# Another order for the attention's steps and for the second MoE stage's first block, the last rows' gate on TensorE, and 11 fewer idle transposes

## The chip, the core and the metric

The kernel runs on one core of one Trainium2 chip. The metric is the device time of one execution in microseconds (us). The core has five engines that run side by side: TensorE (PE in the rows; its weight loads, PEld, have a row of their own), VectorE (DVE), ScalarE (ACT), GpSimd (POOL) and SyncE (SP), which here only issues transfers. Each takes its instructions in the order in which the program lists them and waits for the others through semaphores. Sixteen DMA engines move data.

## The reference

The output of an attention feeds a mixture of experts, whose output feeds a second one:

```python
q_rot, k_rot = rotate(q), rotate(k)           # 4 batches, 8 heads, 576 rows, 64 wide
scores = scale * matmul(q_rot, k_rot.T); scores -= max(scores)
attn = exp(scores); attn /= sum(attn) + 1e-09
x = matmul(attn, v)                           # reordered to 2304 rows of 512

logits = x @ w_gate + modality_bias[modality_id]      # first stage, 8 experts
e = argmax(logits); gate_w = softmax(logits)[e]
x = gate_w * (relu(x @ w1[e]) @ w2[e])                # w1 512x1024, w2 1024x512

do_compute = x @ w_skip > 0                           # second stage
logits = x @ w_gate2; e = argmax(logits); gate_w = softmax(logits)[e]
out = x + where(do_compute, gate_w * (relu(x @ w1_2[e]) @ w2_2[e]), 0)
```

All of it is float32.

## The kernel before, in words

Nearly every product is made of three matmuls: each operand is split into a high and a low part, and high x high, low x high and high x low are added. ScalarE writes the high part (a cast), VectorE the low part (a subtraction); the steps ending in `_hi` and `_lo` and the pieces `split1`, `split2` are these. The low part waits for the high part, and TensorE for both.

**Attention** (`attention`, lines 268 to 690). There are 16 pairs of heads, p = 0 to 15. A pair is loaded, rotated (`rope`, VectorE and GpSimd), transposed (`qk_tr`, L364 and L367), split and stacked. Its scores come in tiles of 128 rows by 576 columns: `s_mm` (L430, four or eight matmuls, two buffers S), `s_max` (L443, VectorE), `s_exp` (L447, ScalarE). The weights of a tile are transposed (`t_mm`, L525) and split (`t_hi` L528, `t_lo` L532), then multiplied with v (`pv`, L559). The finished output O of a head is copied by ScalarE (`o_ev`, L568), turned (`o_mm`, L577), divided by the row sums (`o_norm`, L583; `r_inv`, L480 to L482) and stored (`x_store`, L590 and L592). a and b are the two heads of a pair. After each batch come the routing steps of the first MoE stage (`route…`, `scat…`, which write the experts' lists).

Each step has a position in the table `POS` (L39 to L83). A pair's base is 10 p; all steps of all pairs are sorted by base plus position and issued in that order, so a step's number sets its place in the queue of every engine that it uses. One step may hold several instructions on several queues; a tuple gives one number for each instruction of a TensorE step. The steps at the end of the last pair are already those of the first MoE stage: loads of its first weights (`load1`, `load2`, L1036), splits (`w_hi`, `w_lo`, `w2_hi`, `w2_lo`), transposes (`x_mm`) and the first layer in four hidden parts (`m_mm0` to `m_mm3`, L1115, with relu in `m_hi`, `m_lo`). `keep_warm(n)` (L600) issues n transposes of a constant whose result nobody reads, at the start (36, then 20 and 12 as `warm1` and `warm3`), 8 more as `warm2` and 16 as `warm4`.

**First MoE stage** (`moe1`): blocks of 256 sorted rows of one expert; gather by GpSimd, transposes, first layer, second layer (L1164). Its epilogue `epi(i, t, stage)` treats 128 rows: "out" scales the result y by the gate (ScalarE, L1183); then come the nine logits of the second stage (eight experts and the skip score), made in one of two ways. For some rows GpSimd multiplies with three of the nine weight rows ("prod", L1190), ScalarE sums these ("sums", L1195) and VectorE makes six sums of products (the tuple, L1199). For the others TensorE transposes the rows ("turn", L1206, copied by ScalarE, L1208) and multiplies them with the weights ("gate", L1213). "top" picks the expert (VectorE, with an exponential on ScalarE, L1222), "count" finds its place in the list (L1233, L1234), "list" scatters it. "turn" and the middle of "prod" also scatter the rows to memory.

**Second MoE stage** (`moe2`): blocks of 128 rows, `body(i)`: `mm1` (first layer, L1434), `relu` (L1444), `h_tr` (transposes L1449, split L1452 and L1453), `mm2` (second layer, L1474), `xt` (transposes of the next block's rows), splits of the next weights (`split1`, `split2`), and at the end the residual and the scatter (L1532). The order of the calls in `body` is the order of each queue. Weights of a new expert are loaded and split only where a block needs them (conditional branches). In block 0 alone, `last(t, …)` runs the epilogue of the 256 rows of the first stage's last block (t = 0 and 1) between the block's own steps:

```python
            last(1, "out")
            last(0, "sums", (3, 4, 5), (6, 7, 8))
            mm1(0, range(0, 1))
            last(1, "turn")
```

Buffers are rotated: `rot(name, …)` hands out a buffer again, and the program then waits until its earlier readers are done, DMAs among them.

## Time and profile before

| | us |
|---|---|
| median of 3 runs | 750.29 (750.17 to 752.8) |
| profiled execution, own time | 752.11 |
| its span in the trace | 750.5 |
| TensorE busy | 709.6 (95%) |
| VectorE busy | 548.4 (73%) |
| ScalarE busy | 458.2 (61%) |
| GpSimd busy | 376.3 (50%) |
| mean granted clock of TensorE | 0.979 |

The span is the time from the first to the last record of the trace; what lies around it is 1.6 us here. Shares of busy time are means over three stages: the attention up to about 330 us, the first MoE stage to about 600, the second to the end. A time in brackets in a timeline is how long the engine stood idle ahead of the instruction, and what ended that; clock 1.00 is TensorE's 2.4 GHz, 0.50 would be 1.2 GHz throughout. Matmuls are pipelined, so the busy time of a group of them overlaps that of the next.

### The profile page before, as it was taken

How to read it: one execution, taken by the hardware profiler on the slowest of the kernel's cores; microseconds unless marked ns; L12 is line 12 of the kernel's file. 1: busy time of each engine (PE TensorE's matmuls, PEld its weight loads, DVE VectorE, ACT ScalarE, POOL GpSimd, SP SyncE). 2: the span in 40 equal slices, each digit the busy share in tenths (PEclk: the TensorE clock that was granted, in tenths of full speed). 3: DMA queues.
4: the chain of work that ended last, by engine and by line, in shares of the span. 5: the costliest groups of instructions: out<-in, count | busy, mean ns of one | idle time of the engine just before them, and what ended most of it. 6: DMA issues, size and time to landing. Idle time of an engine off the chain costs nothing. (4 is left out here: it accounts for less than half of the span.)

```text
span 750.5 us, 15355 instructions
## 1 busy us (share of the span) xinstructions
PE 709.6 (95%) x4844; PEld 643.2 (86%) x4844; DVE 548.4 (73%) x1335; ACT 458.2 (61%) x1046; POOL 376.3 (50%) x464
## 2 busy tenths in 40 slices
PE   6899999999999999978999999999998969999995
PEld 6799999999999999978989988998897748777773
DVE  6789999999999999974436544655569773489892
ACT  3788888888888888881223332333255452387881
POOL 7755576759587855244244554254355312123233
PEclk9899999999999999998999999999999989999998
DMA  5665556555656554470411110110677031679910
GB/s 141 129 156 140 127 127 149 130 125 131 155 129 141 137 133 92 103 239 0 128 58 58 57 43 29 43 57 16 170 266 234 22 118 39 249 250 326 331 48 18
DMA packets 76656, 94.68 MB, mean 126 GB/s; under 512 B 29736, under 2 KB 50472, under 8 KB 76547
## 3 DMA queue, kind: packets, MB, share of 16 engines
q1 hardware_dynamic: 67970, 78.22, 37.5%
q0 software_dynamic: 7200, 12.46, 5.3%
q10 hardware_dynamic: 1376, 2.75, 1.1%
q8 instruction: 43, 0.70, 0.4%
q14 instruction: 67, 0.54, 0.3%
HBM read 64.48 MB, written 12.97 MB: 103 GB/s over the span
## 5 line engine op out<-in xcount | busy, mean ns | idle before, releaser
L430 PE MATMUL S<-w1s 128*128 128x288 f32 x640 | 134.1, 323 | 4.0 <-ACT w1s L386 1.3
L1164 PE MATMUL psY<-w2s,hT 128*128 128x512 f32 x480 | 116.0, 396 | 0.0
L1115 PE MATMUL psM<-xT,w1s 128*128 128x256 f32 x864 | 110.6, 286 | 2.6 <-DVE hT L1128 2.6
L1115 PEld LDWEIGHTS psM<-xT,w1s 128*128 128x128 f32 x864 | 106.5, 191 | 3.7 <-DVE hT L1128 3.1
L430 PEld LDWEIGHTS S<-w1s 128*128 128x128 f32 x640 | 98.7, 192 | 8.8 <-ACT PP L447 1.7
L1164 PEld LDWEIGHTS psY<-w2s,hT 128*128 128x128 f32 x480 | 87.9, 188 | 17.3
L447 ACT ACTIVATE PP<-S,nm 128x576 f32<-128x576 f32 x128 | 95.8, 749 | 6.5 <-DVE nm L443 4.4
L443 DVE TENSOR_REDUCE nm<-S 128x1 f32<-128x576 f32 x128 | 94.8, 750 | 3.8 <-PE S L430 3.7
L532 DVE TENSOR_TENSOR tl<-T,th 128x512 fp32r<-128x512 f32 x128 | 88.0, 687 | 12.7 <-ACT th L528 9.4
L525 PE MATMUL T<-ident,PP 128*128 128x128 f32 x512 | 94.3, 274 | 0.8 <-DVE w1s L399 0.4
L528 ACT CAST th<-T 128x512 fp32r<-128x512 f32 x128 | 75.1, 587 | 17.8 <-PE T L525 15.2
L559 PE MATMUL O<-th,vh 128*128 128x288 f32 x256 | 76.4, 332 | 0.9 <-ACT os L568 0.9
L525 PEld LDWEIGHTS T<-ident,PP 128*128 128x128 f32 x512 | 63.9, 140 | 3.4 <-DVE tl L532 1.0
L559 PE MATMUL O<-tl,vh 128*128 128x288 f32 x256 | 64.5, 305 | 0.0
L1434 PE MATMUL psM<-w1s,xT 128*128 128x512 f32 x240 | 63.0, 408 | 1.0 <-DVEq L1351 0.7
L1474 PE MATMUL psY<-w2s,hT 128*128 128x512 f32 x240 | 62.2, 401 | 0.0
L962 POOL DMA_INDIRECT list<-tgs,si x20 | 21.5, 1076 | 80.0 <-issue 40.4
L330 POOL TENSOR_TENSOR mem_w<-qkn,mem_w 128x640 f32<-128x640 f32 x30 | 46.8, 1561 | 20.4 <-PE T L367 20.2
L1128 DVE SCALAR_TENSOR_TENSOR hT<-psM,hT 128x512 fp32r<-128x512 f32 x36 | 24.8, 688 | 43.1 <-ACT hT L1123 43.1
L1434 PEld LDWEIGHTS psM<-w1s,xT 128*128 128x128 f32 x240 | 44.7, 192 | 12.7 <-DVE xT L1101 2.2
L1183 ACT ACTIVATE x<-psY,tg 128x512 f32<-128x512 f32 x20 | 13.8, 689 | 67.7 <-PE psY L1164 56.4
L1101 DVE TENSOR_TENSOR xT<-psT,xT 128x512 fp32r<-128x512 f32 x31 | 20.4, 686 | 44.2 <-ACT xT L1097 43.1
(276 smaller groups left out, 1522.6 us busy)
## 6 DMA issues: line engine op xcount, KB each, us to landing
raw<-in_moe_w_dram SPq DMA_DIRECT2D x24, 512.0 KB
mem_w<-in_moe_w_dram SPq DMA_DIRECT2D x20, 512.0 KB
w1s<-w1s SPq DMA_DIRECT2D x30, 256.0 KB
raw1b<-in_moe_w_dram SPq DMA_DIRECT2D x12, 512.0 KB
raw2b<-in_moe_w_dram SPq DMA_DIRECT2D x12, 512.0 KB
w1s<-w1s SPq DMA_DIRECT2D x16, 288.0 KB
qkn<-in_q_dram SPq DMA_DIRECT2D x16, 256.0 KB
qkn<-in_k_dram SPq DMA_DIRECT2D x16, 256.0 KB
```

The costliest lines, as they stand in the source:

```text
L330: eng.tensor_tensor(r, x, tb[:, i, 0].unsqueeze(1).broadcast_to([128, 2, 5, D]), op=ALU.mult)
L430: yield nc.tensor.matmul(ps[:, hf, 0:288], s["wide"][:, o : o + 128], s["K"][h % 2][:, kk, hf * 288 : hf * 288 + 288], start=first and kk ...
L443: nc.vector.tensor_reduce(st[h // 2]["nm"][:, h % 2, c : c + 1], hs[h]["ps", c][:, :, 0:288], axis=AX.XY, op=ALU.max, negate=True)
L447: nc.scalar.activation(PP[:, c, h % 2 * S : h % 2 * S + S].rearrange("p (a b) -> p a b", a=2), hs[h]["ps", c][:, :, 0:288], AF.Exp, bias=s ...
L525: yield nc.tensor.transpose(ps[:, c * 128 : c * 128 + 128], PP[:, c, o : o + 128], ident)
L528: nc.scalar.copy(hs[h]["th"][:, j, 0:512], hs[h]["tp", j])
L532: nc.vector.tensor_tensor(s["tl"][:, j, 0:512], s["tp", j], s["th"][:, j, 0:512].bitcast(F32), op=ALU.subtract)
L559: yield nc.tensor.matmul(s["ot"][:, hf, 0:288], st[h // 2]["vh"][:, h % 2, j].rearrange("p s d -> p (s d)"), w[:, hf * 288 : hf * 288 + 28 ...
L1115: self.nc.tensor.matmul(ps[:, a], self.w1s[:, wi, dc, fs], x[:, xi, dc], start=(dc == 0 and wi + xi == 0), stop=(dc == 3 and wi == 1))
L1164: nc.tensor.matmul(ps, h[:, hi, f, t * 128 : t * 128 + 128], w2s[:, wi, f], start=(f == 0 and hi + wi == 0), stop=(f == 7 and hi == 1))
L1434: nc.tensor.matmul(ms[hf], x[:, xi, dc], w1s[:, wi, dc, hf * 512 : hf * 512 + 512], start=(dc == 0 and wi + xi == 0), stop=(dc == 3 and xi ...
L1474: nc.tensor.matmul(y, hT[:, hi, f], w2s[:, wi, f], start=(f == 0 and hi + wi == 0), stop=(f == 7 and hi == 1))
```

## The change

Four things change. The table `POS` has new numbers for nearly all steps; names and steps stay. The first `keep_warm` has 25 transposes and not 36, so that with `warm1` and `warm3` 57 stand at the start and not 68. `epi` has two more stages: "last out", which is "out" into a buffer of its own (`x2l`), and "turn only", which is "turn" without the scatter. And `body` calls its steps in another order: the rows t = 0 go through "turn only" and "gate" and no longer through the sums, the eight chunks of `split2(0)` are made as 2, 2 and 4 at three places, and `split1` stands behind `relu(1)` and `h_tr(1)`. The GpSimd products of "prod" for t = 0 are still made, with no reader. Below the change, lines from 1183 on stand one to two lines further down (1183 is 1184, 1208 is 1209, 1444 is 1446), up to eight at the end of `body`.

```diff
@@ -37,49 +37,49 @@
...
-    s_mm2a=(-29.2907, -29.2907, -29.2907, -29.2907), s_max2a=-28.5991, s_exp2a=-28.0836,
-    s_mm3a=(-27.0942, -27.0942, -27.0896, -26.5376), s_max3a=-25.7889, s_exp3a=-24.5167,
-    s_mm0b=(-21.3933, -21.3218, -21.2364, -21.1351), s_max0b=-20.8898, s_exp0b=-20.1501,
...
-    pv3a=(-18.1424, -18.1045, -18.1045, -18.1045), pv4a=(-16.4217, -15.8968), o_eva=-14.5228,
...
-    scat3=16.9444, scat4=19.5742, ahead1=14.2223, ahead2=19.7233, ahead3=29.4759, load1=14.5742, load2=-24.2645,
...
-    const6=29.8505, const2=-1.1138, const3=13.7753, const4=21.8754, const5=-41.303, warm1=-41.3244, warm2=-27.378,
...
+    s_mm2a=(-30.3324, -30.3324, -30.3161, -30.3161), s_max2a=-30.0852, s_exp2a=-29.8453,
+    s_mm3a=(-29.5419, -29.5384, -29.5384, -29.5384), s_max3a=-29.1744, s_exp3a=-25.2003,
+    s_mm0b=(-22.3888, -22.3888, -22.3888, -22.3888), s_max0b=-20.7046, s_exp0b=-20.6509,
...
+    pv3a=(-19.9474, -19.9474, -19.9474, -19.9474), pv4a=(-19.2133, -19.2133), o_eva=-15.6853,
...
+    load2=-10.4519, w_hi0=-14.9829, w_lo0=-12.396, w_hi1=-10.448, w_lo1=2324.1258, w_hi2=-10.6774, w_lo2=-6.7813,
...
+    const4=20.5136, const5=-48.1072, warm1=-45.7988, warm2=-35.009, warm3=-40.5065, warm4=2310.5954, switch=-10.4694,
...
@@ -603,7 +603,7 @@
             warm[0] = pp.tile([128, 2, 512], F32, name="O", bufs=1)
 
         warm_tile()
-        keep_warm(36)
+        keep_warm(25)
         steps = []
 
         def at(base, name, f, *args):
@@ -1178,8 +1178,9 @@
                     s[name] = self.rot(f"{name}_{t}", [128, w], dt, bufs=1)
                 nc.scalar.copy(s["tg"], l[:, t])
                 nc.scalar.copy(s["ti"], l[:, t, 0:1])
-            elif stage == "out":
-                s["x2"] = self.rot(f"x2{t}", [128, DM], bufs=1)
+            elif stage in ("out", "last out"):
+
+                s["x2"] = self.rot(f"x2{t}" if stage == "out" else "x2l", [128, DM], bufs=1)
                 nc.scalar.activation(s["x2"], s["y"], AF.Copy, scale=s["tg"][:, 1:2])
             elif stage == "prod":
 
@@ -1199,14 +1200,15 @@
                     nc.vector.scalar_tensor_tensor(
                         self.junk, s["y"], s["tg"][:, 1:2], self.gw[e], op0=ALU.mult, op1=ALU.mult, accum_out=s["lg"][:, e : e + 1]
                     )
-            elif stage == "turn":
+            elif stage in ("turn", "turn only"):
                 x2 = s["x2"]
                 ps = self.bank("T")
                 for dc in range(4):
                     nc.tensor.transpose(ps[:, dc * 128 : dc * 128 + 128], x2[:, dc * 128 : dc * 128 + 128], self.ident)
                 s["x2t"] = self.rot("x2t", [128, 4, 128], F32)
                 nc.scalar.copy(s["x2t"].rearrange("p c t -> p (c t)"), ps)
-                self.scatter(self.out, s["ti"], x2, N)
+                if stage == "turn":
+                    self.scatter(self.out, s["ti"], x2, N)
             elif stage == "gate":
                 pg = self.bank("G")
                 for dc in range(4):
@@ -1473,48 +1475,54 @@
                     for hi, wi in ((0, 0), (0, 1), (1, 0)):
                         nc.tensor.matmul(y, hT[:, hi, f], w2s[:, wi, f], start=(f == 0 and hi + wi == 0), stop=(f == 7 and hi == 1))
 
-            last(1, "out")
-            last(0, "sums", (3, 4, 5), (6, 7, 8))
+
+            last(0, "turn only")
+            last(1, "last out")
             mm1(0, range(0, 1))
             last(1, "turn")
             if i == 0:
                 self.moe2_second()
+            last(0, "gate", "top")
             mm1(0, range(1, 2))
-            last(0, "top")
             if i == 0:
-                split2(0, range(0, 4))
-            split2(i, range(4, 8))
-            if i + 2 > NA2 + 1:
-                self.seq_load(q, i + 2, 1)
+                split2(0, range(0, 2))
+            else:
+                split2(i, range(4, 8))
+                if i + 2 > NA2 + 1:
+                    self.seq_load(q, i + 2, 1)
+            last(1, "gate", "top")
             mm1(0, range(2, 4))
             relu(0)
-            last(0, "count", "list")
-            last(1, "gate", "top")
             mm1(1, range(0, 2))
+            last(0, "count")
             h_tr(0)
+            last(0, "list")
+            mm1(1, range(2, 4))
+            relu(1)
+            if i == 0:
+                split2(0, range(2, 4))
             split1((0,))
-            mm1(1, range(2, 4))
-            split1((1,))
-            relu(1)
-            last(1, "count")
             if i > 0:
                 fetch(i + 2)
             if i + 3 > NA2:
                 self.seq_list(q, i + 3)
             mm2(range(0, 2))
+            last(1, "count")
+            h_tr(1)
+            split1((1,))
             last(1, "list")
             if i == 0:
+                split2(0, range(4, 8))
 
                 for j in range(NE2, NA2):
                     self.seq_list(q, j)
-            h_tr(1)
-            split1((2, 3))
-            if i + 3 > NA2 + 1:
-                self.seq_load(q, i + 3, 0)
             mm2(range(2, 4))
             if i == 1:
                 tot = self.counts(self.acc2, "d")
             xt(i + 1)
+            split1((2, 3))
+            if i + 3 > NA2 + 1:
+                self.seq_load(q, i + 3, 0)
             mm2(range(4, 8))
             if i == 1:
 
```

Three places show how queues move. Numbers behind a name tell buffers and tiles apart.

ScalarE in a steady pair, head a, before: L528 is the high part of a transposed tile, L447 an exponential of a score tile, L568 the copy of a head's finished output.

```order
L528 CAST th_4633<-T_4645 128x512
L447 ACTIVATE PP_76,sm1_92<-S_4647,nm_4264 128x576
L528 CAST th_4633<-T_4668 128x512
L568 COPY os0_101<-O_4606 128x576
L447 ACTIVATE PP_76,sm1_92<-S_4670,nm_4264 128x576
L528 CAST th_4633<-T_4722 128x512
L447 ACTIVATE PP_76,sm1_92<-S_4717,nm_4264 128x576
```

After:

```order
L528 CAST th_4618<-T_4630 128x512
L447 ACTIVATE PP_76,sm1_92<-S_4633,nm_4265 128x576
L528 CAST th_4618<-T_4650 128x512
L447 ACTIVATE PP_76,sm1_92<-S_4652,nm_4265 128x576
L568 COPY os0_101<-O_4591 128x576
L528 CAST th_4618<-T_4692 128x512
L447 ACTIVATE PP_76,sm1_92<-S_4686,nm_4265 128x576
```

The exponential of the third of these score tiles stands ahead of the copy of the output, and not behind it.

SyncE at the seam from the attention to the first MoE stage, before: L1036 is the load of the first stage's weights (here the last two of the four transfers into `mem_w`, the second layer's), L590 and L592 are the attention's stores.

```order
L1036 ISA
L1036 DMA mem_w_72<-in_moe_w2_dram 128x2x512
L1036 ISA
L1036 DMA mem_w_72<-in_moe_w2_dram 128x2x512
L590 DMA out_0_dram<-xb1_106 512x1x128
L592 DMA out_0_dram<-xb1_106 64x64 x2
L590 DMA out_0_dram<-xb2_107 512x1x128
L592 DMA out_0_dram<-xb2_107 64x64 x2
L590 DMA out_0_dram<-xb0_105 512x1x128
L592 DMA out_0_dram<-xb0_105 64x64 x2
```

After:

```order
L590 DMA out_0_dram<-xb1_106 512x1x128
L592 DMA out_0_dram<-xb1_106 64x64 x2
L590 DMA out_0_dram<-xb2_107 512x1x128
L592 DMA out_0_dram<-xb2_107 64x64 x2
L1036 ISA
L1036 DMA mem_w_72<-in_moe_w2_dram 128x2x512
L1036 ISA
L1036 DMA mem_w_72<-in_moe_w2_dram 128x2x512
L1036 ISA
L1036 DMA mem_w_72<-in_moe_w2_dram 128x2x512
L1036 ISA
L1036 DMA mem_w_72<-in_moe_w2_dram 128x2x512
L590 DMA out_0_dram<-xb0_105 512x1x128
```

The four transfers of the second layer's weights stand behind two stores of the attention, and not ahead of them.

ScalarE in the first block of the second stage, before: `x21` is the buffer of the scaled rows, `psT` a transpose, `w2s` the high part of the second layer's weights, L1444 a relu.

```order
L1183 ACTIVATE x21_0_5294<-psY_1_5149,tg_1_0_5203 128x512
L1195 ACTIVATE x2t_1_5133,lg_0_0_5176<-x2t_1_5133 128x512
L1195 ACTIVATE x2t_0_5132,lg_0_0_5176<-x2t_0_5132 128x512
L1195 ACTIVATE prod_0_5575,lg_0_0_5176<-prod_0_5575 128x512
L1208 COPY x2t_0_5132<-psT_1_5183 128x512
L1222 ACTIVATE e_ex_0_5380,se_1_5383<-e_d_0_5376 128x8
L1013 CAST w2s_4884<-raw2b_5116 128x512 x8
L1444 ACTIVATE x2t_1_5133<-psM_0_5307 128x512
L1240 COPY tgs_2_5429<-tg_0_0_5175 128x1
```

After:

```order
L1209 COPY x2t_0_5121<-psT_1_5172 128x512
L1184 ACTIVATE x2l_0_10892<-psY_1_5138,tg_1_0_5192 128x512
L1209 COPY x2t_1_5122<-psT_0_5171 128x512
L1224 ACTIVATE e_ex_0_5369,se_1_5372<-e_d_0_5365 128x8
L1013 CAST w2s_4877<-raw2b_5105 128x512 x2
L1224 ACTIVATE e_ex_1_5370,se_2_5373<-e_d_1_5366 128x8
L1446 ACTIVATE x2t_0_5121<-psM_0_5296 128x512
L1454 CAST hT_4875<-psT_1_5172 128x4x128
L1242 COPY tgs_2_5418<-tg_0_0_5164 128x1
L1446 ACTIVATE x2t_1_5122<-psM_1_5297 128x512
L1013 CAST w2s_4877<-raw2b_5105 128x512 x2
L1454 CAST hT_4875<-psT_0_5171 128x4x128
```

The copy of the first rows' transpose (now L1209) comes first, the last rows go to `x2l`, the three sums are gone, and the relu (now L1446) comes after two weight chunks and not after eight, but behind a second small exponential (now L1224).

## Rows read from the trace of the kernel before

**Rows 1.** Page, part 1: busy us, share of the span, instructions of each engine

```profile
PE 709.6 (95%) x4844; PEld 643.2 (86%) x4844; DVE 548.4 (73%) x1335; ACT 458.2 (61%) x1046; POOL 376.3 (50%) x464
```

**Rows 2.** Table of stretches: bounds, length, busy us of each engine, clock, DMA share, GB/s

```profile
12.00:28.00 16.00, 10.73 (x52) 9.29 (x53) 9.29 (x18) 8.38 (x23) 12.71 (x11) 0.68 0.36 88
...
49.00:301.00 252.00, 250.54 (x2024) 242.26 (x2023) 228.81 (x467) 222.82 (x519) 171.20 (x215) 1.00 0.57 134
...
343.00:364.00 21.00, 19.11 (x118) 17.19 (x117) 6.54 (x14) 4.57 (x13) 8.24 (x19) 0.92 0.07 15
...
660.00:680.00 20.00, 19.43 (x92) 15.31 (x91) 18.61 (x27) 15.94 (x27) 4.78 (x6) 1.00 0.85 293
```

**Rows 3.** Timeline of all engines, 0 to 17 us: start, duration, engine, line, operation, [idle before]

```profile
1.50 9.27 PE L600 MATMUL O<-ident 128*128 128x128 f32 x68 [1.50 <-POOL ident masks.py:199]
...
8.42 0.82 DVE L336 TENSOR_TENSOR mem_w<-mem_w 128x640 f32<-128x640 f32 x1
...
10.82 0.83 DVE L336 TENSOR_TENSOR mem_w<-mem_w 128x640 f32<-128x640 f32 x1
...
12.45 0.69 DVE L398 TENSOR_TENSOR w1s<-T,w1s 64x512 fp32r<-64x512 f32 x1 [0.81 <-ACT w1s L387]
```

**Rows 4.** Timeline of TensorE, 9 to 28 us

```profile
13.99 0.63 PE L364 MATMUL T<-ident,mem_w 128*128 128x128 f32 x4 [2.02 <-DVE w1s L399]
...
21.68 1.91 PE L600 MATMUL O<-ident 128*128 128x128 f32 x8
...
25.60 1.33 PE L430 MATMUL S<-w1s 128*128 128x288 f32 x8
```

**Rows 5.** Timeline of ScalarE, 219 to 227 us, inside one steady pair

```profile
220.83 0.59 ACT L528 CAST th<-T 128x512 fp32r<-128x512 f32 x1
222.03 0.64 ACT L568 COPY os<-O 128x576 f32<-128x576 f32 x1 [0.61 <-PE O L559]
222.56 0.75 ACT L447 ACTIVATE PP<-S,nm 128x576 f32<-128x576 f32 x1
```

**Rows 6.** Timeline of VectorE in the same stretch

```profile
220.96 0.76 DVE L443 TENSOR_REDUCE nm<-S 128x1 f32<-128x576 f32 x1
```

**Rows 7.** List of waits, 49 to 301 us: waiting and awaited, total us, times, longest

```profile
ACT os L568 <- PE O L559: 8.2, 14, 0.6
...
PEld T L367 <- DVE tl L532: 4.2, 13, 0.3
```

**Rows 8.** Timeline of SyncE's queue, 290 to 345 us

```profile
314.05 2.30 SPq L1036 DMA_DIRECT2D mem_w<-in_moe_w_dram  x4
```

**Rows 9.** Table of stretches of 5 us, columns as in rows 2

```profile
315.00:320.00 5.00, 5.00 (x46) 4.92 (x45) 4.52 (x11) 4.10 (x9) 0.79 (x1) 1.00 1.02 280
```

**Rows 10.** Timeline of GpSimd, 290 to 345 us

```profile
326.19 0.18 POOL L1060 CAST tok<-list 128x2 int32<-128x2 f32 x1 [5.45 <-DMA list<-list]
```

**Rows 11.** Timeline of TensorE, 343 to 356 us

```profile
345.16 0.18 PE L781 MATMUL T<-acc,ones 128*128 128x40 bf16 x1 [1.83 <-POOL acc L763]
...
352.50 1.91 PE L600 MATMUL O<-ident 128*128 128x128 f32 x16
```

**Rows 12.** Timeline of VectorE, 596 to 624 us

```profile
608.89 4.90 DVE L1016 TENSOR_TENSOR w2s<-raw2b,w2s 128x512 fp32r<-128x512 f32 x8
```

**Rows 13.** Timeline of TensorE, 596 to 624 us

```profile
599.41 0.93 PE L1434 MATMUL psM<-w1s,xT 128*128 128x512 f32 x3 [0.72 <-DVEq L1351]
605.50 1.11 PE L1206 MATMUL psT<-ident,x 128*128 128x128 f32 x4 [5.16 <-ACT x L1183]
...
623.17 1.09 PE L1434 MATMUL psM<-w1s,xT 128*128 128x512 f32 x4
```

**Rows 14.** Timeline of ScalarE, 596 to 624 us

```profile
604.76 0.69 ACT L1183 ACTIVATE x<-psY,tg 128x512 f32<-128x512 f32 x1 [10.50 <-DMA out_dram<-x,ti]
...
607.98 4.25 ACT L1013 CAST w2s<-raw2b 128x512 fp32r<-128x512 f32 x8
```

**Rows 15.** Timeline of GpSimd, 596 to 624 us

```profile
600.56 1.27 POOL L1190 TENSOR_TENSOR prod<-x,raw1b 128x512 f32<-128x512 f32 x1
```

74 lines of the change are left out of this document (37 added, 37 removed).

## The prediction

> **What bounds the kernel now.** Read first the busy times of the page, then the table of stretches, then the timelines of the places that the diff touches. On the page TensorE is busy for 95% of the span [rows 1], so only its waits and its half-clock time can be won, and what other engines do matters where it makes TensorE wait. The table of stretches says where that is. In the steady attention (49 to 301 us) TensorE's matmuls stand at 250.54 of 252 us, its weight loads at 242.26; VectorE and ScalarE fill 229 and 223 of it [rows 2]. So three engines are nearly full there, and 1.5 us (by the matmuls) to 9.7 us (by the weight loads) can be had at most. The open places are the start (clock 0.68 between 12 and 28 us), the seam from attention to the first MoE stage (clock 0.92 in 343 to 364), and the first block of the second MoE stage, where TensorE stands through one long wait (part 4). The clocks are in [rows 2] as well. In the later blocks of that stage TensorE has 19.43 and VectorE 18.61 of 20 us [rows 2]: full again.
>
> All working is in microseconds of the profiled execution. It ran 752.11 (span 750.5), 0.24% above the median of 750.29; I take the differences off the median. A measurement of this kernel tells 0.5%, 3.75 us, from no change.
>
> **1. Start.** Before, 68 idle transposes run from 1.50 to 10.77, 0.136 each, and q's transposes stand behind them though q's rotation ends at 9.24 [rows 3]. 11 fewer end it 1.5 earlier, at 9.27; q's part then comes 1.3 earlier. k's part does not: its rotation ends at 11.65 in either kernel. VectorE's subtraction at 12.45, which waited 0.81 for ScalarE's copies of q, can now follow that rotation at once, so k's transposes come 0.8 earlier than 13.99 [rows 3, 4]. The second edit: the eight idle transposes at 21.68, which stand between two score tiles and take 1.1 (eight at 0.136) to 1.9 (their row), now stand ahead of the first one, where TensorE waits for k anyway. Eight score matmuls stood at 25.60 [rows 4]; Of the 1.1 to 1.9 I take 1.3, since the clock is below full there, and so put these 0.8 + 1.3 = 2.1 earlier, rounded to **-2.0**. Ends: -0.8 if the idle ones cost as much in the new place, -2.7 if all of their 1.9 goes. If the cover there is gone, they cost that 1.3.
>
> **2. Steady attention.** The operations are the same; 15 pairs of heads follow at about 19 us each. Three orders move on the three engines: ScalarE takes the exponential of the third score tile ahead of the copy of the finished output, VectorE takes that tile's maximum ahead of the reciprocals, and TensorE issues most score tiles as four matmuls on end. In the row, ScalarE stands 0.61 waiting for the output at 222.03, with the exponential right behind it though that tile's maximum ended at 221.72 [rows 5, 6]. Over the stretch this wait occurs 14 times, 8.2 in sum, and TensorE's for the low part of the transposed weights 13 times, 4.2 in sum [rows 7]. ScalarE's gain is not all TensorE's: TensorE can win 9.7 in 13.3 pairs, 0.73 per pair, and much of it is waits on the two-buffer pace of the score tiles that merely come later in the pair. I take a third of it, 0.25 x 15 = 3.75, rounded to **-3.5**: nearer to the weight loads' end than the matmuls', since the 14 ScalarE waits are what the edit takes away. Ends: 0 and -7; a loss is priced as a rival.
>
> **3. Seam.** Before, the second weight load (four DMAs, SyncE 314.05) stands straight behind the first and ahead of the attention's last stores; the DMA engines are at 1.02 of their time in 315 to 320, and GpSimd waits 5.45 for a list that it reads there [rows 8 to 10]. Now the load stands behind the stores of two more thirds, so these land earlier and the list meets less traffic. Then on TensorE: the second half of the routing is moved up in VectorE's order, so its wait of 1.83 for GpSimd's counts at 345.16 [rows 11] should vanish, and the 16 idle transposes (1.91 at 352.50) stand ahead of the last hidden block and not behind it; the clock of 0.92 there means 3.4 half-clock us of 21, of which one such stretch follows that wait [rows 2, 11]. Against that, VectorE now splits all eight pieces of the second weights ahead of the low part of the last first-layer piece, and the last hidden block waits for it, which I put at one piece, about 0.6 (4.90 for eight [rows 12]), to 1.2. Sum: -1.8 for the wait, -1.7 for half of the 3.4, +0.8 = **-2.7**. Ends: -4 (the gathers come earlier as well) and +1 (neither the clock nor the gathers gain, and the second weights land late).
>
> The row shows the transfers sharing one resource. The Trainium skill, page "DMA: Bandwidth & Descriptors", section "Issuing engines are not separate DMA queues", states the same and draws the other side: transfers of all engines interleave on the same 16 DMA engines. By that rule the moved load does not vanish but meets the gathers that follow the list instead, and this term would be worth at most the 1.8 of the routing wait less 0.8; no row of the kernel before shows the load in its new place.
>
> The code of the first MoE stage is the same and full, so what is won ahead of it carries through to 599.
>
> **4. First block of the second MoE stage.** This is the surest term. At 604.76 ScalarE writes the last 128 rows into a buffer that a scatter is still reading: it waits 10.50 for that DMA, while TensorE, after three matmuls at 599.41, waits 5.16 for the rows to transpose; the next block starts at 623.17 [rows 13, 14]. After, the rows go into a buffer of their own (x2l) and wait for no DMA. What is late next is ScalarE's copy of the earlier rows' transpose, now ahead of it: it overwrites a tile that GpSimd's products use, which end at 601.83 [rows 15]. So: copy 601.9 to 602.6, write of the last rows to 603.3 (0.69 as in [rows 14]), transposes from 603.3 where they stood at 605.50: **2.2 earlier**. The new gate on TensorE (4 transposes and 4 small matmuls, under the 1.11 of four transposes each) lies in the wait; six VectorE passes and three ScalarE sums go. ScalarE's eight weight copies, 4.25 from 607.98 and ahead of the first relu [rows 14], become 2, 2 and 4: relu comes after two of them and a second, short exponential that needs the second gate, about 608.3. That second gate is the **new wait**: queued behind it on ScalarE are relu, the first hidden transpose and so TensorE's second product. Hidden transpose about 609, first layer done 610.8, third quarter of the second product from 614, its last pieces paced by VectorE's splits at 0.61 each [rows 12], end 618 to 619.5 where 623.17 stood: **-4.0**. Ends: -2.5 and -5.5. GpSimd's scatters, lists and gathers of the next blocks start from the same rows and shift by about as much, so I leave the gain standing.
>
> **5. Later blocks.** Relu and hidden transpose no longer stand behind VectorE's and ScalarE's weight splits, but VectorE's sum (18.61 of 20 [rows 2]) is unchanged. The load of the first weights is issued some 4 later. I take **-1**; ends -3 (half a us in six blocks) and +1.5.
>
> **Sum:** -2.0 - 3.5 - 2.7 - 4.0 - 1.0 = -13.2; 750.3 - 13.2 = 737.1.
>
> **Rivals.**
> A. *The pace of the steady attention holds.* With VectorE and ScalarE at 229 and 223 of 252 [rows 2] and the score tiles in two buffers, the wait taken from ScalarE comes back one tile later; term 2 is 0 and the seam gives half. 750.3 - 8.3 = 742. For it: the matmul row leaves just 1.5 us. Against: the 14 waits are real.
> B. *ScalarE's copy is held as before.* If the copy of the first transpose must wait for the scatter too, it starts at 604.8, the rows at 605.4, and only the removed sums and the weight copies are won: term 4 falls to -1.5. 739.6. Against: the copy reads a transpose and writes a tile that only GpSimd's products use.
> C. *The moved load meets the gathers* (the rule in part 3): the seam is worth -1 to +1, taken as 0, and the rest stands: 739.8.
> D. *Slower: bursts of four score matmuls.* One score tile of eight matmuls takes 1.33 [rows 4], and ScalarE needs 0.75 + 0.59 [rows 5] and an accumulator read per tile, about 1.5. Issued on end with four transposes between (about 1.0 from tile to tile, estimated from that row of score matmuls), each of the two heads could wait 0.5 more for a free score buffer: 1.0 x 15 pairs = +15 in place of -3.5. 750.3 - 9.7 + 15 = 755.6. It decides from 0.65 per pair on, where it eats the other terms. Against: the bursts come where the buffers are free, and TensorE has the products with v to fill in.
> E. *More than a third*: the waits of part 2 and the seam go whole: -7 and -4, so 732.
>
> **How the numbers follow.** Forecast as summed (734 to 740) 0.50, A 0.20, B 0.07, C 0.06, D 0.06, E 0.08, and 0.03 that two of these losses come together near 748. Likeliest: 737.1. The range, 731 to 746, leaves out D, part of E and the last. Faster by over 0.5% (below 746.5): 0.91 less a little for the width of A and C, 0.89; within 0.5%: 0.06; slower (above 754): 0.05.
>
> **What would show it.** Start: the eight score matmuls at about 23.6, the idle ones ahead of the first score tile. Steady: pairs at 18.7 to 18.8, the ScalarE wait for the output gone from the list of waits. Seam: no wait at the routing's second count; first matmul of the second layer about 2.7 earlier against the last pair of heads. First block: ScalarE's copy at about 2.5 after the first matmul of the block and not 5.4, block length about 19.5 to 20 and not 23.8. Wrong it is if pairs take 19 or more (A, D), if ScalarE still waits for a DMA in that block (B), or if the later blocks are longer than before by as much as the first is shorter.

## The result, and the profile after

The changed kernel is slower: 758.81 us median of 12 runs (753.56 to 763.25) against 750.94 (749.29 to 753.23), a ratio of 1.0097 with a 95% interval of 1.0075 to 1.0119. The same kernel, in two further comparisons on two chips, gave 1.0031 (1.0015 to 1.0047) and 1.0045 (1.0026 to 1.0063). All three stand above 1; the prediction of 737.1 and its range of 731 to 746 were wrong.

The profiled execution took 755.46, its span 753.8. First the page's busy times, then the stretches of [rows 2] in after (bounds, length, busy us of TensorE, its weight loads, VectorE, ScalarE and GpSimd, clock, DMA share, GB/s):

```profile
PE 709.3 (94%) x4845; PEld 640.6 (85%) x4845; DVE 546.6 (73%) x1324; ACT 455.4 (60%) x1041; POOL 381.4 (51%) x464
```

```profile
12.00:28.00 16.00, 10.90 (x58) 9.35 (x58) 11.06 (x22) 8.93 (x24) 12.94 (x12) 0.79 0.38 96
49.00:301.00 252.00, 247.51 (x1998) 237.48 (x1997) 227.04 (x460) 217.76 (x513) 169.93 (x215) 1.00 0.54 131
...
343.00:364.00 21.00, 19.81 (x126) 17.44 (x124) 10.20 (x28) 5.68 (x15) 7.81 (x15) 1.00 0.29 71
...
600.00:620.00 20.00, 16.84 (x73) 13.54 (x72) 9.67 (x42) 9.36 (x22) 3.53 (x4) 0.74 0.32 111
```

TensorE's busy time is that of [rows 1], and the span is 3.3 longer: waits were added. The clock rose where the prediction wanted it, at the start (0.68 to 0.79) and the seam (0.92 to 1.00), and fell at 600 to 620, where the kernel before has 0.83. In the steady attention TensorE does 3.0 less work in the same 252 us.

The two traces, marked at the same instructions, give this account. A pair is timed from the four transposes (L538) of one pair to those of the next.

| place | before | after | gain (-) or loss, predicted | measured |
|---|---|---|---|---|
| start, to the first pair's L538 | 35.58 | 34.44 | -2.0 | -1.14 |
| fifteen pairs | 285.42 | 288.11 | -3.5 | +2.69 |
| seam, to the first L1164 | 33.94 | 30.11 | -2.7 | -3.83 |
| first MoE stage, to the first matmul of the second | 244.47 | 246.80 | 0 | +2.33 |
| first block of the second stage | 23.76 | 23.09 | -4.0 | -0.67 |
| the rest of it, to the last matmul | 117.79 | 121.63 | -1.0 | +3.84 |

The sum is +3.2; the spans differ by 3.3. The other 3.4 between this execution and the median of its 12 runs has no trace, and no run here explains it.

**The pairs.** The loss is not spread. Twelve of the 15 pairs take 0.01 to 0.2 less than before, eight of them about 0.1 (18.81 to 18.90 for 18.95 to 19.01). Pair 7 takes 21.75, pair 3 19.97 and pair 4 19.04. TensorE of after in pair 7, with its one wait for these copies:

```profile
152.78 0.77 PE L430 MATMUL S<-w1s 128*128 128x288 f32 x4 [2.74 <-DMA w1s<-w1s]
```

L430 are the next pair's first scores; the transfer that they wait for is one of the ten copies on SyncE (`stackq`, `stackk`, `stack2`, L402) that bring q and k into place. SyncE's queue there, before and then after:

```profile
139.23 5.68 SPq L402 DMA_DIRECT2D w1s<-w1s  x8
144.96 0.61 SPq L590 DMA_DIRECT2D out_dram<-xb  x1
145.61 1.68 SPq L592 DMA_DIRECT2D out_dram<-xb  x2
147.39 1.20 SPq L402 DMA_DIRECT2D w1s<-w1s  x2
```

```profile
139.80 2.48 SPq L402 DMA_DIRECT2D w1s<-w1s  x4
142.33 0.66 SPq L590 DMA_DIRECT2D out_dram<-xb  x1
143.03 1.31 SPq L592 DMA_DIRECT2D out_dram<-xb  x2
144.78 8.43 SPq L402 DMA_DIRECT2D w1s<-w1s  x6
```

`x_store` went from 1.9574 to -0.5661 in the table, and so three stores stand between q's four copies (`stackq`) and k's four (`stackk`) and not behind both; `stack2`, the last two, stood behind the stores before as well. Before, k's copies were issued by 144.9; now they start at 144.78. The last copy that the first scores need lands 0.9 to 4.4 us ahead of them before, 0.1 to 3.4 after, and in pair 7 too late.

Pair 3 has another cause. The table also moves `const3`, two comparisons of VectorE on 128 x 20 numbers (L247), from pair 4 into pair 3, ahead of a score tile's maximum. VectorE and TensorE of after:

```profile
85.49 1.64 DVE L247 TENSOR_SCALAR sel<-mf 128x20 f32<-128x20 f32 x2
```

```profile
88.97 0.66 PE L525 MATMUL T<-ident,PP 128*128 128x128 f32 x4 [0.88 <-DVE tl L532]
```

Before, the two took 0.24 together, at 98.28, while GpSimd stood idle; at 85.49 GpSimd works on its part of a rotation (L330, L334). Of the 13 traces with the new table, eight have both comparisons long (0.77 to 0.82 and 0.90 to 0.91) and a pair 3 of 19.93 to 19.97; five have the second one at 0.16 and a pair 3 of 19.18 to 19.21.

**The seam.** TensorE and SyncE of after, for [rows 11] and [rows 8]:

```profile
342.90 0.18 PE L781 MATMUL T<-acc,ones 128*128 128x40 bf16 x1
...
349.46 2.90 PE L1115 MATMUL S<-xT,w1s 128*128 128x256 f32 x22 [1.16 <-DVE w1s L1004]
```

```profile
325.10 2.26 SPq L1036 DMA_DIRECT2D mem_w<-in_moe_w_dram  x4
```

The wait of 1.83 ahead of L781 is gone, GpSimd's wait for the list [rows 10] fell from 5.45 to 3.04, and the half-clock time went whole: the granted clock is at 2.4 GHz from 321 to 364, where before it stood at 1.2 from 336.0 to 339.4 and from 346.2 to 349.6. The wait that the prediction added is there (1.16 for 0.8). How much the seam gives differs from trace to trace: it takes 31.77 to 33.94 in the four with the old table and 28.81 to 30.11 in the 13 with the new one, before and after being the longest of each.

**The first MoE stage** does not carry the gain. The lead of 2.3 is still 2.2 at 541 and is gone at 599. In between ScalarE issues the second stage's `w2` load. ScalarE before:

```profile
539.67 6.50 ACTq L1036 DMA_DIRECT2D raw2b<-in_moe_w_dram  x4
547.56 0.59 ACT L1097 CAST xT<-psT 128x512 fp32r<-128x512 f32 x1 [8.21 <-PE psM L1115]
```

ScalarE after:

```profile
538.74 6.23 ACTq L1036 DMA_DIRECT2D raw2b<-in_moe_w_dram  x4
546.85 0.58 ACT L1097 CAST xT<-psT 128x512 fp32r<-128x512 f32 x1 [9.71 <-DMA raw2b<-in_moe_w_dram]
```

TensorE was 2.2 earlier there, but the issues ended only 1.2 earlier (544.97 for 546.17), ScalarE's next casts stand behind them, and TensorE waits 0.31 for ScalarE at 548.08. From the last transposes ahead of this place (541.41 in after) to the second stage's first matmul, the four traces with the old table take 55.26 to 55.85 and the 12 with the new one and this load on ScalarE 56.13 to 59.32, after itself 58.05. So the loss of 2.3 is this execution's: the changed kernel's other two traces (`e5`, `e9`) take 56.70 and 56.37.

**The first block of the second stage.** ScalarE and TensorE of after, for [rows 14] and [rows 13]:

```profile
601.53 0.58 ACT L1209 COPY x2t<-psT 128x512 f32<-128x512 f32 x1 [7.71 <-POOLq L1353]
```

```profile
602.76 1.11 PE L1207 MATMUL psT<-ident,x2l 128*128 128x128 f32 x4 [2.35 <-ACT x2l L1184]
603.66 1.72 PE L1215 MATMUL psG<-wg2s,x2t 128*128 128x9 f32 x8
605.23 1.63 PE L1436 MATMUL psM<-w1s,xT 128*128 128x512 f32 x3
606.65 1.71 PE L1215 MATMUL psG<-wg2s,x2t 128*128 128x9 f32 x8
608.22 4.83 PE L1436 MATMUL psM<-w1s,xT 128*128 128x512 f32 x12
...
622.54 2.73 PE L1436 MATMUL psM<-w1s,xT 128*128 128x512 f32 x11
```

The DMA wait is gone and TensorE goes on at 602.76, where 605.50 stood: 2.7 earlier. But the clock is at 1.2 GHz from 601.9 to 612.1 (before: 602.2 to 609.0, half of it in the wait), and the block ends 0.6 earlier.

**The later blocks.** Blocks that take new weights last 13.66 to 14.54, and 13.23 to 13.69 before. ScalarE before and then after, from the cast of the next block's rows (686.18 and 686.61) on, and TensorE after:

```profile
686.66 4.26 ACT L1013 CAST w2s<-mem_w 128x512 fp32r<-128x512 f32 x8
691.07 0.60 ACT L1444 ACTIVATE x2t<-psM 128x512 f32<-128x512 f32 x1 [0.15 <-issue]
```

```profile
687.34 2.00 ACT L1000 CAST w1s<-raw1b 128x1024 fp32r<-128x1024 f32 x2
689.24 4.26 ACT L1013 CAST w2s<-mem_w 128x512 fp32r<-128x512 f32 x8
693.40 0.58 ACT L1446 ACTIVATE x2t<-psM 128x512 f32<-128x512 f32 x1
```

```profile
694.04 0.66 PE L1451 MATMUL psT<-ident,x2t 128*128 128x128 f32 x4 [0.52 <-ACT x2t L1446]
```

`split1((2, 3))` now stands behind `xt(i + 1)`, so its two casts run right ahead of the eight of `w2s`, and the relu that TensorE needs comes behind all ten.

The second block, which takes no new weights, lost too: 13.55 for 12.51. TensorE of after waits there for the gather of the third block's rows, a wait that before does not have:

```profile
632.82 0.66 PE L1094 MATMUL psT<-ident,xh 128*128 128x128 f32 x4 [0.85 <-DMA xh<-out_dram,tok]
```

Every trace with the first block's new order has this wait (0.79 to 0.97), and none with the old order.

### The profile page after: what moved, and what is told of

It reads as the page before. It is cut to its first block, busy times and chain, and to the rows that moved or that the text cites. A ratio compares the mean times of both kernels' runs of the same rounds, so it can differ in the third digit from the quotient of the medians.

```text
span 753.8 us, 15266 instructions
## 1 busy us (share of the span) xinstructions
PE 709.3 (94%) x4845; PEld 640.6 (85%) x4845; DVE 546.6 (73%) x1324; ACT 455.4 (60%) x1041; POOL 381.4 (51%) x464
## 5 line engine op out<-in xcount | busy, mean ns | idle before, releaser
L430 PE MATMUL S<-w1s 128*128 128x288 f32 x640 | 119.3, 312 | 6.0 <-DMA w1s<-w1s 2.7
L1164 PE MATMUL psY<-w2s,hT 128*128 128x512 f32 x480 | 116.0, 396 | 0.0
L447 ACT ACTIVATE PP<-S,nm 128x576 f32<-128x576 f32 x128 | 95.8, 749 | 12.2 <-DVE nm L443 10.6
L1164 PEld LDWEIGHTS psY<-w2s,hT 128*128 128x128 f32 x480 | 87.9, 188 | 17.3
L430 PEld LDWEIGHTS S<-w1s 128*128 128x128 f32 x640 | 92.4, 190 | 9.9 <-issue 3.0
L528 ACT CAST th<-T 128x512 fp32r<-128x512 f32 x128 | 75.0, 586 | 27.3 <-PE T L525 21.6
L559 PE MATMUL O<-th,vh 128*128 128x288 f32 x256 | 74.6, 331 | 0.8 <-ACT os L568 0.8
L1476 PE MATMUL psY<-w2s,hT 128*128 128x512 f32 x240 | 64.0, 404 | 2.9 <-DVE hT L1455 1.8
L330 POOL TENSOR_TENSOR mem_w<-qkn,mem_w 128x640 f32<-128x640 f32 x30 | 46.9, 1564 | 16.3 <-PE T L367 13.0
L1476 PEld LDWEIGHTS psY<-w2s,hT 128*128 128x128 f32 x240 | 43.1, 188 | 14.1 <-DVE hT L1455 3.9
L334 POOL TENSOR_TENSOR mem_w<-qkn,mem_w 128x320 f32<-128x320 f32 x60 | 51.0, 872 | 1.3 <-DVE mem_w L336 1.3
```

The costliest lines, as they stand in the source:

```text
L334: eng.tensor_tensor(t2r[:, :, :, a : a + 32], x[:, :, :, o : o + 32], sn, op=ALU.mult)
L430: yield nc.tensor.matmul(ps[:, hf, 0:288], s["wide"][:, o : o + 128], s["K"][h % 2][:, kk, hf * 288 : hf * 288 + 288], start=first and kk ...
L447: nc.scalar.activation(PP[:, c, h % 2 * S : h % 2 * S + S].rearrange("p (a b) -> p a b", a=2), hs[h]["ps", c][:, :, 0:288], AF.Exp, bias=s ...
L528: nc.scalar.copy(hs[h]["th"][:, j, 0:512], hs[h]["tp", j])
L559: yield nc.tensor.matmul(s["ot"][:, hf, 0:288], st[h // 2]["vh"][:, h % 2, j].rearrange("p s d -> p (s d)"), w[:, hf * 288 : hf * 288 + 28 ...
L1164: nc.tensor.matmul(ps, h[:, hi, f, t * 128 : t * 128 + 128], w2s[:, wi, f], start=(f == 0 and hi + wi == 0), stop=(f == 7 and hi == 1))
```

## The experiments

Each ratio is to the kernel before on the same chip; kernels told under one heading were not always on one chip.

### The table alone, and all but the table

`e1_pos_only` is the kernel before with the new table:

```diff
-    load=-40.2545, rope0=-39.1031, rope1=-38.1966, v_hi=-28.3147, v_lo=-23.8684,
+    load=-41.2173, rope0=-40.5708, rope1=-40.4422, v_hi=-29.9666, v_lo=-25.2209,
...
```

> The kernel before with the new table POS alone (36 first idle transposes, old second stage). Theory S (the stacking copies, line 402, now get to SyncE behind a store and land 0.1 to 2.6 us ahead of the score matmuls that read them, where 0.9 to 4.4 stood before; when one lands late TensorE waits for it): the waits for w1s copies in the steady pairs are there as in the changed kernel, runs spread over 6 us or more, median 752 to 757. Theory B (bursts of four score matmuls are slow by themselves): pairs would take over 19.0 us in every pair, spread below 4 us. If neither, the attention is not the cause: 745 to 748 (start and seam gain 4 to 5).

1.0012 (0.9996 to 1.0028). Pair 7 takes 23.25, with the same line in the list of waits (2.7, once); the seam takes 28.83; the first block 25.09; later blocks are as before.

`e2_old_pos` is the changed kernel with the table of before (the reverse diff).

> The changed kernel with the old table POS: only 25 first idle transposes and the second stage's new order and gate are left. If the later blocks of the second stage lose what the two traces show (3.8 us from the second block's start to the end, relu(0) behind more weight casts on ScalarE) and the first block gains 0.7: 752.5 to 754.5. By theory S the spread of the runs goes back to about 4 us; if the spread stays at 10, the second stage is what varies.

1.0059 (1.004 to 1.0078). The pairs take 19.00 (the first 19.72) and none waits for the copies; the first block takes 23.29, later ones 13.63 to 14.07. So the table by itself pays for its wait with the seam. In `e2_old_pos` the way from the second block to the last matmul is 3.5 longer than in before (121.27 for 117.79), the start 1.0 and the pairs 0.7: most of the loss is the second stage's order. Why the first block, unaltered in `e1_pos_only`, took 1.3 more there than in before, no run tells.

### The stores of x

`e3_store_late`, and a second time on another chip as `e10_store_late_2`, is the changed kernel with one number back; `e5_after_again` and `e9_after_third` are the changed kernel as it is.

```diff
-    t_mm4=(-20.3729, -20.3729, -20.3729, -20.3729), t_hi4=-20.0186, t_lo4=-19.8578, r_inv=-10.7013, x_store=-0.5661,
+    t_mm4=(-20.3729, -20.3729, -20.3729, -20.3729), t_hi4=-20.0186, t_lo4=-19.8578, r_inv=-10.7013, x_store=1.9574,
```

> The changed kernel with x_store alone put back to 1.9574, so that the store stands behind the stacking copies on SyncE and not between them. Theory S: the copies land about 2 us earlier against the scores, no wait for w1s in the steady pairs, median 750 to 752, spread under 5. Theory B and any cause in the second stage: 757 to 760 as before, spread 10.

> The changed kernel, unaltered, beside the next three on one chip. If its 758.8 is the kernel's own: 756 to 760, with runs from 752 to 763. If much of it was that chip: 751 to 755. Its profile shows which waits a second execution has: by theory S the pair at 150 to 172 us again waits 2 to 5 us for the stacking copies.

> The changed kernel unaltered, a third chip job, as the base of the next one. So far it stood at 1.0097 and 1.0031 of the kernel before. Theory S: one pair (150 to 172 us) takes 21.5 us or more for want of the stacking copies; 752 to 759.

> The changed kernel with x_store alone back at 1.9574, beside the changed kernel on the same chip. Theory S: 2 to 4 us under it (more on a chip where copies land later), that pair at 19.0 to 19.3 us. If the place of the store does not matter: the same within 1 us.

With the number back: 0.9997 (0.9983 to 1.001) and 0.9999 (0.9979 to 1.0019). Without: 1.0031 and 1.0045, pair 7 at 21.52 and 22.50. SyncE in `e3_store_late` and TensorE's first scores there:

```profile
139.28 10.25 SPq L402 DMA_DIRECT2D w1s<-w1s  x10
```

```profile
149.20 0.77 PE L430 MATMUL S<-w1s 128*128 128x288 f32 x4
```

All ten copies go first and no wait is left: pair 7 takes 19.00 and 18.87. `e9` and `e10` shared a chip: 0.0046 of 749.83 us, 3.4 us, is what the place of three stores costs, with an uncertainty of about 2 from the two intervals. Pair 7 alone takes 3.6 more in `e9` than in `e10` (22.50 for 18.87), of which TensorE's wait ahead of the first scores is 2.0.

`e14_before_store_between` puts only the stores between the copies, in the kernel before:

```diff
-    t_mm4=(-19.6242, -19.6242, -19.6242, -19.6242), t_hi4=-18.9706, t_lo4=-17.4754, r_inv=-11.2088, x_store=1.9574,
+    t_mm4=(-19.6242, -19.6242, -19.6242, -19.6242), t_hi4=-18.9706, t_lo4=-17.4754, r_inv=-11.2088, x_store=-0.12,
```

> The kernel before with one number of the attention's order changed: x_store from 1.9574 to -0.12, so that on SyncE the two stores of x are issued between the stacking copies, and nothing else of the new table is taken. Theory S (the place of the stores on SyncE's queue alone makes the wait of the score matmuls for the stacked weights): a wait of PE L430 for DMA w1s of 1 to 3 us appears in pair 7, pair 7 takes 20 to 23 us where before takes 19.00, and the total is 1 to 3 us over before (ratio 1.001 to 1.004). Rival O (the store hurts only together with the new order of TensorE and VectorE, which needs the copies earlier): no such wait, pair 7 at 19.0, total within 0.5 us of before.

1.0021 (1.0003 to 1.0039), between the two. Pair 7 takes 18.99 and no wait for the copies is in the list; but in six pairs the copies land under 1 us ahead of the scores, and the fifteen pairs take 286.06 for 285.42. (A wait of 0.33 ahead of the scores at 188.95 is listed for VectorE; the copies land 0.13 ahead there, so it may be theirs.) Theory S, that the store makes the wait of 1 to 3 us by itself, falls in this trace: the store uses up the copies' lead. What more it takes is not shown. In pair 7 the last of k's copies landed 2.9 after its issue had ended here (146.69 to 149.58) and 4.6 in after (148.01 to 152.65), and no run tells why.

### The later blocks

`e4_later_old` gives blocks from 1 on their old order; block 0 keeps the new one. The core of it:

```diff
+            if i > 0:
+                split1((0,))
...
+            if i == 0:
+                split1((1,))
+            else:
+                split1((2, 3))
...
-            split1((2, 3))
+            if i == 0:
+                split1((2, 3))
```

> The changed kernel with the old places of split1, relu(1), h_tr(1) and the first weights' load in all blocks of the second stage but the first. If the later blocks' loss is from ScalarE's pieces 2 and 3 behind xt, the blocks with new weights go from 13.8 back to 13.4 us and the median falls by 2.5 to 4 (755 to 756.5), the spread staying at 8 or more (theory S). If the loss is from GpSimd's lists and gathers, the blocks stay at 13.8 and the time at 758 to 759.

1.0014 (0.9995 to 1.0032), though pair 7 waited 3.3 for the copies in its profile. From the fourth on the blocks take 13.05 to 13.68 again; the second still takes 13.67. TensorE in the block whose like waits 1.23 in after (`680.23`, ahead of L1451), and after itself:

```profile
678.10 0.60 PE L1451 MATMUL psT<-ident,x2t 128*128 128x128 f32 x4
```

```profile
680.23 0.66 PE L1451 MATMUL psT<-ident,x2t 128*128 128x128 f32 x4 [1.23 <-ACT x2t L1446]
```

`e6_store_and_later` has both edits, `e3` and `e4`.

> x_store back at 1.9574 and the later blocks' old order together. If the two losses are separate places (theory S for the pairs, ScalarE's casts for the later blocks), their gains add: about 3.5 below the kernel with x_store alone put back (749.1), so 744 to 747, 0.4 to 0.8% below the kernel before. If the later blocks are paced by GpSimd's gathers, the earlier arrival is lost again: 748 to 750.

0.9944 (0.9922 to 0.9966): faster than before. On its chip the changed kernel was at 1.0031, so the two edits are worth 6.5 us; with 3.4 for the stores, the later blocks' order costs about 3.1. The traces say the same without the noise of the totals: from the second block to the last matmul, 121.14 to 121.63 in the six with the changed later order and 118.24 to 118.93 in the seven with the old one behind a changed first block.

### The half clock in the first block

`e7_busy_in_wait` is `e6` with 18 idle transposes in the wait of block 0, behind the three matmuls of `mm1(0, range(0, 1))`:

```diff
+            if i == 0:
+                for _ in range(18):
+                    nc.tensor.transpose(y[:, 0:128], self.ident, self.ident)
```

> The kernel with both places put back, and in the second stage's first block 18 idle transposes behind the first three matmuls, where TensorE waits 2.3 us for the last rows. Theory C (the first block gained 0.7 and not 4 because TensorE idles ahead of it and then runs at half clock from 602 to 612): the half-clock stretch goes or gets shorter, the block falls from 23.0 to between 18.5 and 21, the time by 2 to 4.5. Rival (the block is paced by VectorE's and ScalarE's chain, gate, top, relu): the block stays at 22.5 to 23.5 whatever the clock does.

0.9897 (0.988 to 0.9913), 742.35 us: the best version with `e13`, 7.4 us under before. TensorE in that block:

```profile
596.16 2.13 PE L1484 MATMUL psY<-ident 128*128 128x128 f32 x18
598.55 0.66 PE L1207 MATMUL psT<-ident,x2l 128*128 128x128 f32 x4 [0.26 <-ACT x2l L1184]
599.05 0.96 PE L1215 MATMUL psG<-wg2s,x2t 128*128 128x9 f32 x8
599.86 0.94 PE L1436 MATMUL psM<-w1s,xT 128*128 128x512 f32 x3
600.64 0.95 PE L1215 MATMUL psG<-wg2s,x2t 128*128 128x9 f32 x8
601.45 3.06 PE L1436 MATMUL psM<-w1s,xT 128*128 128x512 f32 x12
...
614.17 1.09 PE L1436 MATMUL psM<-w1s,xT 128*128 128x512 f32 x4
```

The same matmuls as in after take 0.96, 0.94, 0.95 and 3.06 for 1.72, 1.63, 1.71 and 4.83, and the block takes 18.79, by the prediction's mechanism and even under its 19.5 to 20. The granted clock is 1.00 from 596 to 616, and 0.74 there in `e6`. The Trainium skill, page "TensorE: Matmul & The Clock Gate", section "Part 4: PE-mode transpose", says that the full clock does not engage in TensorE's transpose mode. The transposes here did hold it; the trace lists them as matmuls with an identity and does not tell in which mode they run.

`e12_before_busy` fills the wait of the kernel before in the same way, with 38:

```diff
+            if i == 0:
+                g = self.bank("G")
+                for _ in range(38):
+                    nc.tensor.transpose(g[:, 0:128], self.ident, self.ident)
```

> The kernel before with 38 idle transposes behind the first three matmuls of the second stage's first block, where TensorE waits 5.2 us. Theory C: the half-clock stretch of 602 to 609 goes, the work of 605.5 to 609 runs at full clock, the block falls from 23.8 by 1 to 2 us (21.8 to 22.8) and the time by as much; the rest of the 5 us between it and the 18.8 of the changed block with transposes is what the new order and gate give. If the block falls to 20 or less, the new order gives next to nothing.

1.0003 (0.9989 to 1.0017): nothing, where I had expected a gain. The half-clock stretch is gone and the block takes 23.81:

```profile
603.61 0.66 PE L1206 MATMUL psT<-ident,x 128*128 128x128 f32 x4 [1.02 <-ACT x L1183]
...
607.16 0.17 PE L1233 MATMUL psG<-oh,U 128*128 128x8 bf16 x1 [0.79 <-DVE oh L1230]
```

In the old order ScalarE and VectorE set the pace, and a faster TensorE waits; a second wait for VectorE, 1.73 at 614.68, stands as it did in before. So the new order alone is worth 0.4 to 1.0 in the block (22.77 to 23.31 in nine profiles, for 23.76), the clock alone 0, and both together 5.0. Of these 5.0 the second block, with its wait for a gather, gives back 1.1 (13.63 in `e7` for 12.51).

### Three reasons tried on the best version

`e8_load2_back` is `e6` with the second weight load back in its old place.

```diff
-    load2=-10.4519, w_hi0=-14.9829, w_lo0=-12.396, w_hi1=-10.448, w_lo1=2324.1258, w_hi2=-10.6774, w_lo2=-6.7813,
+    load2=-24.2645, w_hi0=-14.9829, w_lo0=-12.396, w_hi1=-10.448, w_lo1=2324.1258, w_hi2=-10.6774, w_lo2=-6.7813,
```

> The kernel with both places put back, and load2 back at -24.2645, so that the second weight load stands straight behind the first on SyncE, ahead of the store before last. If the seam's gain of 3.9 is from the moved load: the first transposes come 1 to 2.5 later against the last pair and the time rises by 1 to 3. If it is from TensorE's and VectorE's order alone (routing moved up): no change within 0.5 us.

0.9959 (0.9945 to 0.9974), and the seam takes 28.8 in both. No gain of the moved load shows, and the totals differ by less than their intervals.

`e11_copy_first` is `e7` with ScalarE's copy of the output ahead of the exponential, as before the change; `e15_old_act_dve` puts VectorE's reciprocal back as well.

```diff
-    pv3b=(-14.0898, -13.0816, -12.3965, -12.3965), pv4b=(-10.7441, -10.6576), o_evb=-10.5662,
+    pv3b=(-14.0898, -13.0816, -12.3965, -12.3965), pv4b=(-10.7441, -10.6576), o_evb=-10.655,
```

```diff
-    t_mm4=(-20.3729, -20.3729, -20.3729, -20.3729), t_hi4=-20.0186, t_lo4=-19.8578, r_inv=-10.7013, x_store=1.9574,
+    t_mm4=(-20.3729, -20.3729, -20.3729, -20.3729), t_hi4=-20.0186, t_lo4=-19.8578, r_inv=-10.706, x_store=1.9574,
```

> The kernel with both places put back and 18 idle transposes in the first block's wait (742.35), with o_evb at -10.655: ScalarE copies the finished output ahead of the exponential, as in the kernel before; nothing else moves on any engine. If that order gave the 0.11 us per pair (18.88 against 18.99), the undisturbed pairs return to 18.97 to 19.01. If the gain is from TensorE's order (four score matmuls on end), they stay at 18.86 to 18.91.

> The version of e11 (ScalarE's copy ahead of its exponential, as before the change) with r_inv put back too, so that on VectorE the reciprocal stands where it did before; of the new steady order only TensorE's is left. Theory P (TensorE's order gives the 0.11 us per pair): undisturbed pairs stay at 18.85 to 18.92. Rival V (VectorE's order gives it): they go back to 18.98 to 19.02.

`e11`: 0.9909 (0.9877 to 0.9941). `e15`: 741.59 us in its single run. ScalarE's wait for the output is back in `e11` and absent in after. The lists of waits, 49 to 301 us, of after and then of `e11`:

```profile
ACT th L528 <- PE T L525: 17.7, 41, 0.8
```

```profile
ACT th L528 <- PE T L525: 8.4, 28, 0.4
ACT os L568 <- PE O L559: 8.0, 13, 0.6
```

Yet undisturbed pairs take 18.86 to 18.91 in all of them. In after the wait had only changed its name. In `e15` ScalarE and VectorE go through a steady pair in the order of before, but for routing steps, and the place of the stores makes no difference to these pairs (18.87 to 18.90 in after and in `e3` alike). What gives the 0.11 is the one order left, TensorE's.

`e13_load_on_sync` is `e7` with the `w2` load of 538.74 issued by SyncE.

```diff
-        e = self.reg(q.first["meta"][0:1, 0:1], [ET.Activation], E - 1)
-        self.load(q.slots[1][which], q.w[which], e, self.nc.scalar, (c,))
+        e = self.reg(q.first["meta"][0:1, 0:1], [ET.SP], E - 1)
+        self.load(q.slots[1][which], q.w[which], e, self.nc.sync, (c,))
```

> The version of e7 with one edit: the first second-stage w2 load (L1396, four transfers into raw2b) is issued from SyncE's queue and not from ScalarE's, with the register it reads on SyncE. Theory Q (what was won ahead of the first MoE stage is lost around 540 to 563 because ScalarE stands behind the issues of this load: 532.02 for 9.47 us in e7, and the next cast of xT starts 11.08 us after ScalarE's last work, with the TensorE waiting 1.68 us for it): ScalarE's issue block at about 532 is gone, the stretch from the ninth to the tenth group of x transposes falls from 23.69 to 20 to 21.5 us, and the total is 739 to 740.5 (ratio about 0.986). Rival D (the transfers themselves are the limit, with DMA at 0.9 to 1.0 of its time busy from 530 to 550, and whoever issues waits for the same bytes): the stretch stays within 1 us of 23.7 and the total is 742 to 743. Rival T (SyncE, blocked instead, issues its own later loads late): 743 to 746.

ScalarE and TensorE in `e7`, then SyncE and TensorE in `e13`:

```profile
532.02 9.47 ACTq L1036 DMA_DIRECT2D raw2b<-in_moe_w_dram  x4
542.86 0.58 ACT L1097 CAST xT<-psT 128x512 fp32r<-128x512 f32 x1 [11.08 <-DMA raw2b<-in_moe_w_dram]
```

```profile
544.09 0.66 PE L1207 MATMUL psT<-ident,x 128*128 128x128 f32 x4 [1.68 <-ACT x L1184]
```

```profile
532.36 6.83 SPq L1036 DMA_DIRECT2D raw2b<-in_moe_w_dram  x4
```

```profile
542.26 0.60 PE L1207 MATMUL psT<-ident,x 128*128 128x128 f32 x4
```

From the ninth to the tenth group of x transposes, the stretch fell from 23.69 to 19.50, and TensorE waits for ScalarE no more: the issuing queue is where `e7` lost the gain. From the transposes at 536.06 to the second stage's first matmul `e13` takes 55.46, as the traces with the old table do. But it is one trace, and the total is 0.9898 (0.9873 to 0.9923), no better than `e7`. The stretch took 21.76 in `e6`, 21.04 in `e11` and 20.41 in `e15`, all with the load on ScalarE; `e7` has the slowest, and 1.5 of it are matmuls that ran at 1.2 GHz behind the wait (546.2 to 549.7). What the queue costs in the median of runs stays open.

## Why the prediction was wrong, point by point

1. **Start.** Right in kind, half the size: 1.14 for 2.0. The step that failed is "its rotation ends at 11.65 in either kernel". VectorE before and then after:

```profile
9.90 0.89 DVE L334 TENSOR_TENSOR mem_w<-qkn,mem_w 128x320 f32<-128x320 f32 x2
```

```profile
9.90 2.23 DVE L334 TENSOR_TENSOR mem_w<-qkn,mem_w 128x320 f32<-128x320 f32 x2
```

With fewer idle transposes q's part came earlier, so GpSimd began its first rotation product at 10.25 and not at 11.50, and one of VectorE's two products beside it took 1.83 for 0.48. k's transposes came at 14.57 and not 0.8 before 13.99; the eight score matmuls stood at 24.29 for 25.60 all the same, with the idle transposes ahead at 15.23. In five of the 13 traces with 25 idle transposes (`e3`, `e4`, `e6`, `e7`, `e11`) GpSimd began at 10.90 or later, none of VectorE's steps was long, and the first L538 stands at 33.39 to 33.78, the forecast 2.0 earlier. In the other eight GpSimd began by 10.61, one step of VectorE was long, and it stands at 34.44 to 35.22, with the old table (`e2`) at 36.58. With 36 transposes no step is long, and it stands at 35.52 to 36.74.
2. **Steady attention.** The step that failed most. The prediction followed the three engines that compute and looked at SyncE only at the seam; the table moves `x_store` ahead of `stackk` in every pair. The two tables show it, and the view of [rows 8], read at 139 to 148 us, shows the copies that it now stands ahead of. It cost 3.4 us by `e9` and `e10`. The term's own reason fell too: 0.11 per pair and not 0.25, from TensorE's order and not ScalarE's (`e11`, `e15`). And of the 1.3 or so that 0.11 gives in 12 pairs, pair 3 takes back up to 1.0 (`const3`): with the stores put back, the fifteen pairs take 285.24 and 285.28 (`e3`, `e10`) for 285.42, next to no gain. Rival A priced the missing gain at 742; rival D's mechanism, a wait for free score buffers, did not come.
3. **Seam.** Right, and more than forecast: 3.8 for 2.7, since both half-clock stretches went and not half of them. The wait for the routing left as told. No part of the moved load shows in it (`e8`), so rival C had nothing to decide; that the order of TensorE and VectorE gives it is what is left, and no run takes that order back by itself.
4. **"What is won ahead of it carries through to 599."** False here: 2.2 were won by 541 and none at 599. TensorE was full, but one load held ScalarE's queue, and it began only 0.9 earlier. `e13` shows the place. The size is this trace's: in `e5` and `e9` the stage takes 0.5 and 0.1 more than in before, and not 2.3.
5. **First block.** The mechanism was right to 0.5 us (the transposes at 602.76 for 603.3), and rival B did not come. The missing term was the clock: a shorter wait was still one after which the clock fell, and work that had stood behind the old wait now ran at 1.2 GHz. `e7` shows the 5.0 that the order is worth at 2.4. The last step of the term, that scatters, lists and gathers "shift by about as much", failed too: the second block waits 0.85 for a gather and takes 1.0 more.
6. **Later blocks.** Wrong sign: +3.8 for -1, of which 1.0 is the second block's. The prediction freed the relu from the splits ahead of it in its own block and did not follow `split1((2, 3))` into the next one, where it stands ahead of that block's relu (`e4`: about 3.1).

The forecast put 0.05 on slower, for rival D alone. Three costs that it had not priced, 3.4, 3.1 and the clock's 3.3 (`e6` to `e7`, on one chip), came together; the totals alone give each of them to no better than 2 or 3 us.

## What to carry to other kernels

When a table reorders steps, follow every queue that a step touches through one whole repeat, the transfer queues first: three small stores ahead of a copy cost more here (3.4) than 15 pairs of better order gave (under 1.7). Work moved to the end of a block is work ahead of the next block's first step. And a wait that is shortened but not closed can leave TensorE's clock down for the work that comes behind it; filling it with idle matmuls pays only where no other engine sets the pace.

## What the runs showed of the hardware that was not expected

Issuing the four transfers of a weight load held ScalarE's queue for 4.8 to 9.5 us in the 16 traces that have it there (the DMA engines were busy 0.82 of the time at 530 to 550 in after and 0.95 in `e7`), and ScalarE did nothing else in that time. Some of VectorE's steps took far longer in the traces where GpSimd worked beside them: 0.48 became 1.83 and 0.82 became 2.04 at the start, and 0.17 became 0.77 to 0.91 in pair 3. Eight small matmuls of nine columns take 0.96 us at 2.4 GHz and 1.72 at 1.2 GHz. And one kernel stood 0.31 to 0.97% above the kernel before in three comparisons, further apart than their intervals allow; the cause was not found.
